# Attention and feed-forward emitted in the program's own order, one group of rows per step, instead of an order set by a scheduler

## The chip, the core and the metric

One core of a Trainium2 chip (four computing engines, here called PE for TensorE, DVE for VectorE, ACT for ScalarE and POOL for GpSimd, and SP, which only issues DMAs). The metric is device time in microseconds of one run of the whole program.

## What is computed

```python
# attention, B=4 batches, H=12 heads, S=448 rows, D=64
scores = q @ k.T / 8                       # per head
scores = einsum('bhij,hg->bgij', scores, w_pre)    # heads mixed before the softmax
attn   = softmax(scores)                           # exp(x - max) / (sum + 1e-9)
attn   = einsum('bhij,hg->bgij', attn, w_post)     # heads mixed after it
x      = (attn @ v)                        # to 1792 tokens x 768
# first feed-forward, d_ff 1536
x = (sigmoid(x @ w_gate) * (x @ w_val)) @ w_out
# second feed-forward, d_ff 2048
x = relu(x @ w_in) ** 2 @ w_out2
```

## The kernel before, in words

`attention` cuts each batch's 448 rows into four tiles (120, 120, 120 and 88 rows) and each tile into groups of ten rows: 12, 12, 12 and 9 groups, 45 a batch, 180 in all. Ten rows of twelve heads fill 120 partitions, so that one matmul mixes the heads of a whole group. Two tiles are a chunk. The work on TensorE is:

- `scores(n, p)`, 96 times: two heads of tile n against all keys, side by side in two halves of the array (64 rows of weights each); ACT copies the two results to `e`, and DMAs on SP's queue lay them out anew in `g`, rows by heads (two DMAs for a tile of 120 rows, four for one of 88).
- `premix(s)`, 180 times: one fp32 matmul of 448 columns, two passes in the trace; DVE takes the row maximum, `exponent(s)` on ACT makes exp and its sum, `normal(s)` takes two short steps on DVE and one on POOL (`wn`, the mixer scaled by 1/sum).
- `postmix(s)`, 180 times: four matmuls of 120 columns (eight passes); DVE copies the result into `ap` (`mixed`).
- `values(c, h)`, 48 times: two heads of a chunk, 240 or 208 columns, 16 passes in the other split of the array (64 columns each); ACT copies the result, and a DMA stores it to `xs`.

Premix uses two PSUM banks (`ps_m`), scores two (`ps_q`), postmix and values share four (`ps_b`). In the program a loop over `s` takes one group a step: premix of s, exponent of s-1, normal of s-2, postmix of s-3 or older, and scores of the next tile spread over the tile's steps. The work behind (postmix and values, the list `back`) is paced by a credit: `QUOTA` a step, `PW` or `VW` off it for each item.

That program order is only advice in the kernel before. Up to the end of attention the framework's scheduler puts each engine's instructions in an order of its own; `latest` and `issue_after` tie some instructions behind others. `mlp`, the feed-forward part, is a generator that attention feeds: for the last 40 groups (`EARLY`) it yields, and `whole` takes a step of `mlp` for each (weights loaded, split in parts that TensorE multiplies as fp32r: `w_bias`, `w_high`, `w_low`, `w_sum`, `w_round`, `w_rest`; then the activations `xh`, `xl`). What is left of `mlp` after attention is already emitted in the program's order (`manual_schedule`). It has 4896 matmuls of 448 columns (line 597), 36 for each block of weights.

Of the kernel before, what the change touches and what calls it, by code (L numbers as in the profile page):

```python
# [13 lines left out]
PSUM = bass.MemoryType.PSUM  # L14
DRAM = bass.MemoryType.DRAM

E = mybir.EngineType

P = 128
JP = 112  # L20
GI = 10
HV = 4
LAG = 3
LA = 3
NA = 8
PW, VW, QUOTA = 0.86, 1.6, 1.6
KB = 10
EARLY = 40
EM = 2
EACH = (1, 3, 2)  # L30
BEHIND = (E.Activation, E.DVE, E.Pool)


def row_tiles(S):
# [11 lines left out]
def attention(tc, q, k, v, w_pre, w_post, xs, B, H, S, D):  # L46
# [31 lines left out]
    with ExitStack() as ctx, ExitStack() as mid, ExitStack() as left:  # L78
# [15 lines left out]
        wp = one.tile([KM, GI, H], F32, name="wp")  # L94
        wq = one.tile([KM, H, GI], F32, name="wq")

        def mixers():
            wr = p0.tile([KM, 2, H], F32, name="wr")
            mask = p0.tile([KM, GI, H], F32, name="mask")
            for n, w in enumerate((w_pre, w_post)):  # L100
                nc.sync.dma_start(out=wr[:, n, :], in_=w.unsqueeze(0).to_broadcast([GI, H, H]))
            nc.gpsimd.memset(mask, 1.0)
            for base, mult in ((0, 1), (H - 1, -1)):
                nc.gpsimd.affine_select(
                    out=mask,
                    in_=mask,
                    compare_op=ALU.is_ge,
                    fill=0.0,
                    base=base,
                    pattern=[[-mult * H, GI], [0, H]],  # L110
                    channel_multiplier=mult,
                )
            nc.vector.tensor_tensor(
                out=wp, in0=mask, in1=wr[:, 0:1, :].to_broadcast([KM, GI, H]), op=ALU.mult
            )
            nc.vector.tensor_scalar(out=wp, in0=wp, scalar1=SCALE, scalar2=None, op0=ALU.mult)
            nc.vector.tensor_tensor(
                out=wq.rearrange("p g i -> p i g"),
                in0=mask,
                in1=wr[:, 1:2, :].to_broadcast([KM, GI, H]),  # L120
                op=ALU.mult,
            )
# [19 lines left out]
        def scores(n, p):  # L142

            b, i0, isz = tiles[n]
            if p == 0:
                g_t[n] = pg.tile([KM, GT, S], F32, tag="g", name="g")
            kt = k_t.pop((b, p)) if i0 + isz == S else k_t[b, p]
            ps = [
                ps_b.tile([P, S], F32, tag="b", name="ps_s")
                if n == 0 and p % 2  # L150
                else ps_q.tile([P, S], F32, tag="q", name="ps_s")
                for _ in range(2)
            ]
            for o in range(2):
                r = slice(o * D, (o + 1) * D)
                nc.tensor.matmul(  # L156
                    ps[o][:isz], lhsT=q_t[n][r, p, :isz], rhs=kt[r], start=True, stop=True
                )
            e = p4.tile([IM, 2, S], F32, tag="e", name="e")
            ng, rest = divmod(isz, GI)  # L160
            to = g_t[n].rearrange("(r h) g j -> h r g j", h=H)
            for o in range(2):
                if n == 0 and o:
                    nc.vector.tensor_copy(e[:isz, o], ps[o][:isz])
                else:
                    nc.scalar.copy(e[:isz, o], ps[o][:isz])  # L166
                for r0, r1, g in ((0, rest, ng + 1), (rest, GI, ng)):
                    if r0 < r1:
                        e0 = r0 * (ng + 1)
                        nc.sync.dma_start(  # L170
                            out=to[2 * p + o, r0:r1, :g], in_=e[e0 : e0 + (r1 - r0) * g, o]
                        )
# [4 lines left out]
        def premix(s):  # L177
            n, r0, rows = groups[s][:3]
            kk = rows * H
            ps = ps_m.tile([P, S], F32, tag="m", name="ps_m")  # L180
            w = wp.rearrange("p i g -> p (i g)")
            nc.tensor.matmul(  # L182
                ps[:kk], lhsT=w[:kk, :kk], rhs=g_t[n][:kk, r0 // GI], start=True, stop=True
            )
            nm = pa.tile([KM, 1], F32, tag="nm", name="nm")
            nc.vector.tensor_reduce(out=nm[:kk], in_=ps[:kk], op=ALU.max, axis=AX.X, negate=True)  # L186
            a_t[s] = [ps, nm]
# [86 lines left out]
        def load_next(load, order):  # L274
            x = next(order, None)
            if x is not None:
                load(*x)


        front = {s: [] for s in range(NG)}  # L280
        for n in range(1, NT):
            lo_, hi_ = starts[n - 1], starts[n] - LA
            for p in range(NP):
                front[lo_ + (hi_ - lo_) * p // NP].append((n, p))

        front_used = [s for s in front if front[s]]
        back = []
        for c, ch in enumerate(chunks):
            back += [(postmix, PW, s) for s in range(ch[3], ch[4])]
            back += [(values, VW, c, h) for h in range(0, H, 2)]  # L290
        bpos, credit = 0, 0.0

        def flush():
            now, pending[:] = list(pending), []
            for f, *x in now:
                f(*x)

        for p in range(0, NP, 2):
            q_load(0, p, p + 2)
            load_next(k_load, k_order)  # L300
            load_next(k_load, k_order)
        mixers()
        q_load(1)
        for p in range(NP):
            scores(0, p)
        with ExitStack() as behind:
            for ins in latest(tc, (mybir.EngineType.SP,)):
                behind.enter_context(tc.issue_after(ins))
            for _ in range(2):
                load_next(v_load, v_order)  # L310
            for _ in range(KB - NP):
                load_next(k_load, k_order)
        for s in range(NG + 30):
            if s < NG:
                premix(s)
            flush()
            if 1 <= s <= NG:
                exponent(s - 1)
            if 2 <= s < NG + 2:
                normal(s - 2)  # L320
            for n, h in front.get(s, ()):
                scores(n, h)
                if tiles[n][1] + tiles[n][2] == S:
                    load_next(k_load, k_order)
                if h == NP - 1 and n + 1 < NT:
                    q_load(n + 1)
            credit = min(credit, 0.0) + QUOTA
            fresh = None
            while bpos < len(back) and (credit > 0 or s >= NG):
                f, cost, *x = back[bpos]  # L330
                if f is postmix:
                    if x[0] > s - LAG:
                        break
                    fresh = groups[x[0]][3]
                elif x[0] == fresh:
                    if s < NG:
                        break
                    flush()
                if len(pending) > 3:
                    g, *y = pending.pop(0)  # L340
                    g(*y)
                f(*x)
                if f is values and (x[1] + 2) % HV == 0:
                    load_next(v_load, v_order)
                bpos += 1
                credit -= cost
                if f is postmix and x[0] == NG - 1:
                    flush()
                    mid.close()
                if s >= NG:  # L350
                    yield 3 if bpos == len(back) or back[bpos][0] is values else 2
            if s == max(front_used):
                left.close()
            if NG - EARLY <= s < NG:
                yield 1 if s < max(front_used) else 2
        flush()


# [337 lines left out]
@with_exitstack  # L696
def whole(ctx, tc, q, k, v, w_pre, w_post, wg, wv, wo, wi2, wo2, out):
    B, H, S, D = k.shape[0], 2 * k.shape[1], k.shape[3], k.shape[2] // 2
    DM = out.shape[0]
    dram = ctx.enter_context(tc.tile_pool(name="dram", bufs=1, space=DRAM))  # L700
    xs = [dram.tile([DM, S], F32, name=f"xs{b}") for b in range(B)]
    feed = mlp(tc, xs, wg, wv, wo, wi2, wo2, out, DM, wg.shape[0] * P, wi2.shape[0] * P)
    need = next(feed)
    for given in attention(tc, q, k, v, w_pre, w_post, xs, B, H, S, D):
        for _ in range(EACH[given - 1]):
            if need <= given:
                with ExitStack() as behind:
                    for ins in latest(tc, BEHIND):
                        behind.enter_context(tc.issue_after(ins))
                    need = next(feed)  # L710
    with tc.manual_schedule():
        for _ in feed:
            pass


def latest(tc, engines):

    found = {}
    for ins in reversed(tc.nc.cur_bb.bb.instructions):
        if ins.engine in engines and ins.engine not in found:  # L720
            found[ins.engine] = ins
            if len(found) == len(engines):
                break
    return list(found.values())


# [42 lines left out]
```

## Time and profile before

| what | us |
|---|---|
| median of 3 runs | 1574.31 (1571.27 to 1574.97) |
| the profiled execution | 1571.23 |
| its span in the profile | 1569.5 |
| from the start to the unbroken run of feed-forward matmuls | 604.74 |
| that run, 4714 of the 4896 | 961.25 |

A busy time of TensorE says little here: its matmuls are pipelined and the end of each is modelled, so two that follow with a small gap still look joined. What tells is the distance from the start of one piece to the start of the next.

### The profile page before, as it was taken

How to read it: one execution, taken by the hardware profiler on the slowest of the kernel's cores; microseconds unless marked ns; L12 is line 12 of the kernel's file. 1: busy time of each engine (PE TensorE's matmuls, PEld its weight loads, DVE VectorE, ACT ScalarE, POOL GpSimd, SP SyncE). 2: the span in 40 equal slices, each digit the busy share in tenths (PEclk: the TensorE clock that was granted, in tenths of full speed). 3: DMA queues.
4: the chain of work that ended last, by engine and by line, in shares of the span. 5: the costliest groups of instructions: out<-in, count | busy, mean ns of one | idle time of the engine just before them, and what ended most of it. 6: DMA issues, size and time to landing. Idle time of an engine off the chain costs nothing.

```text
span 1569.5 us, 21157 instructions
## 1 busy us (share of the span) xinstructions
PE 1510.5 (96%) x7848; PEld 1223.4 (78%) x7848; DVE 772.8 (49%) x1275; ACT 541.9 (35%) x1102; POOL 506.8 (32%) x403
## 2 busy tenths in 40 slices
PE   7889999899998899999999999999999999999999
PEld 3546555565554588999999999999999999999998
DVE  3535545473474648877888998961111100333000
ACT  3443444444453433333234443322222211333111
POOL 1211112121132335545455555542222222222221
PEclk8999999999999999999999999999999999999999
DMA  6334525244353334544444445641112121111221
GB/s 211 123 107 134 148 90 179 88 125 129 106 166 103 121 117 163 181 163 160 162 152 170 161 151 188 219 165 62 53 49 61 51 61 51 51 53 54 77 78 42
DMA packets 79530, 185.41 MB, mean 118 GB/s; under 512 B 11204, under 2 KB 48452, under 8 KB 79428
## 3 DMA queue, kind: packets, MB, share of 16 engines
q1 hardware_dynamic: 79428, 184.07, 36.4%
q8 instruction: 62, 1.02, 0.3%
q14 instruction: 40, 0.33, 0.1%
HBM read 107.75 MB, written 37.75 MB: 93 GB/s over the span
## 4 chain that ended last, share of the span: by engine, by line
PE 61%; DMA 0%; DVE 0%; POOL 0%; issue 0%; ACT 0%; ACTq 0%; DVEq 0%; SPq 0%; POOLq 0%
PE ps L597 61%; DMA w_raw<-in_wv 0%; POOL w L457 0%; POOL wl L470 0%; DVE w_t L439 0%; ACT w_f L417 0%; DVE w_f L446 0%; DVE w L426 0%; DVE w_t L423 0%; ACT o L629 0%; DVE ps L615 0%; DVEq L426 0%; ACTq L629 0%; SPq L407 0%; POOLq L457 0%
## 5 line engine op out<-in xcount | busy, mean ns | idle before, releaser
L470 POOL TENSOR_TENSOR wl<-w,wh 128x768 fp32r<-128x768 f32 (+1 forms) x140 | 259.3, 1854 | 543.8 <-ACT wh L464 537.8
L597 PE MATMUL ps<-xh,wl 128*128 128x448 f32 x960 | 350.9, 366 | 1.3 <-POOL wl L470 1.3
L597 PE MATMUL ps<-xh,wh 128*128 128x448 f32 x960 | 351.3, 366 | 0.1
L597 PE MATMUL ps<-xl,wh 128*128 128x448 f32 x960 | 350.9, 365 | 0.0
L597 PE MATMUL ps<-hh,wl 128*128 128x448 f32 x672 | 246.8, 367 | 0.0
L597 PE MATMUL ps<-hl,wh 128*128 128x448 f32 x672 | 246.8, 367 | 0.0
L597 PE MATMUL ps<-hh,wh 128*128 128x448 f32 x672 | 246.6, 367 | 0.0
L205 POOL TENSOR_SCALAR wn<-wq,sm 120x120 f32<-120x120 f32 x180 | 106.0, 589 | 427.3 <-DVE sm L203 256.4
L182 PE MATMUL ps_m<-g,wp 120*120 120x448 f32 x360 | 173.5, 580 | 29.3 <-ACT a L194 15.5
L220 PEld LDWEIGHTS ps_p<-wn,a 120*112 120x112 f32 (+1 forms) x1440 | 160.0, 177 | 49.0 <-issue 40.4
L597 PEld LDWEIGHTS ps<-xh,wl 128*128 128x128 f32 x960 | 180.3, 188 | 16.4 <-POOL wl L470 1.8
L597 PEld LDWEIGHTS ps<-xh,wh 128*128 128x128 f32 x960 | 180.3, 188 | 15.6 <-issue 0.6
L597 PEld LDWEIGHTS ps<-xl,wh 128*128 128x128 f32 x960 | 180.3, 188 | 14.8 <-issue 0.3
L186 DVE TENSOR_REDUCE nm<-ps_m 120x1 f32<-120x448 f32 x180 | 112.2, 623 | 145.4 <-PE ps_m L182 140.3
L194 ACT ACTIVATE a<-ps_m,nm 120x448 f32<-120x448 f32 x180 | 114.0, 633 | 197.0 <-DVE nm L186 126.4
L220 PE MATMUL ps_p<-wn,a 120*112 120x120 f32 (+1 forms) x1440 | 168.8, 269 | 3.1 <-POOL wn L205 2.8
L457 POOL TENSOR_TENSOR w<-w,w_f 128x768 f32<-128x768 f32 (+1 forms) x70 | 135.2, 1932 | 60.1 <-DVE w_f L446 60.1
L232 DVE COPY ap<-ps_p 112x480 f32<-112x480 f32 x180 | 117.1, 652 | 53.5 <-PE ps_p L220 47.8
L156 PE MATMUL ps_s<-k,q 64*120 64x448 f32 (+1 forms) x384 | 124.3, 614 | 15.1 <-ACT e L166 10.4
L597 PEld LDWEIGHTS ps<-hh,wh 128*128 128x128 f32 x672 | 126.1, 188 | 11.6
L597 PEld LDWEIGHTS ps<-hl,wh 128*128 128x128 f32 x672 | 126.1, 188 | 11.6
L597 PEld LDWEIGHTS ps<-hh,wl 128*128 128x128 f32 x672 | 126.1, 188 | 11.6
(39 smaller groups left out, 1291.8 us busy)
## 6 DMA issues: line engine op xcount, KB each, us to landing
g<-e SPq DMA_DIRECT2D x144, 210.0 KB
ws<-w SPq DMA_DIRECT2D x58, 384.0 KB
w<-ws SPq DMA_DIRECT2D x58, 384.0 KB
w_raw<-in_wo SPq DMA_DIRECT2D x18, 768.0 KB
w_raw<-in_wi SPq DMA_DIRECT2D x16, 768.0 KB
vraw<-in_v SPq DMA_DIRECT2D x24, 448.0 KB
w_raw<-in_wg SPq DMA_DIRECT2D x12, 768.0 KB
w_raw<-in_wv SPq DMA_DIRECT2D x12, 768.0 KB
```

The lines of the kernel that those rows point to most:

```text
L156: nc.tensor.matmul(ps[o][:isz], lhsT=q_t[n][r, p, :isz], rhs=kt[r], start=True, stop=True)
L182: nc.tensor.matmul(ps[:kk], lhsT=w[:kk, :kk], rhs=g_t[n][:kk, r0 // GI], start=True, stop=True)
L186: nc.vector.tensor_reduce(out=nm[:kk], in_=ps[:kk], op=ALU.max, axis=AX.X, negate=True)
L194: nc.scalar.activation(a[:kk], ps[:kk], AF.Exp, bias=nm[:kk], accum_out=sm[:kk])
L205: nc.gpsimd.tensor_scalar(out=wn[:kk], in0=wq[:kk], scalar1=sm[:kk], scalar2=None, op0=ALU.mult)
L220: nc.tensor.matmul(ps[:JP, jt], lhsT=a[:kk, jt * JP : (jt + 1) * JP], rhs=wn[:kk].rearrange("p g i -> p (g i)"), start=True, stop=True,)
L232: nc.vector.tensor_copy(ap[c][:, :, :, g0 - i0 : g0 - i0 + rows], ps[:JP, :, :, :rows])
L457: nc.gpsimd.tensor_tensor(out=x[:, s], in0=x[:, s], in1=fs.pop(n)[:, s], op=ALU.add)
L470: nc.gpsimd.tensor_tensor(out=lo[:, s], in0=w32.pop(n)[:, s], in1=h[:, s].bitcast(F32), op=ALU.subtract)
L597: nc.tensor.matmul(ps, lhsT=a, rhs=x, start=first and n == 0, stop=last and n == total - 1)
```

## The change

All of attention and the feed-forward part go under `manual_schedule`: each engine takes its instructions in the order in which the program emits them. The program's loop is laid out for that. The row maximum (`maximum`) is emitted after the copies of the step before. A step has a budget of `STEP` = 2.55, of which premix takes `MW`; scores of the next tile take `SW` where they are due, at most one a step, and one at the end of a step if there is room; the rest goes to postmix and values as long as over 0.5 is left. The load of `vraw` is held back to the next step's start. `mlp`'s early steps begin 64 groups before the end, one in every third step, until the scores are done. Nine buffers for the softmax's tiles instead of eight. `latest` and its ties are gone. The arithmetic is the same.

```diff
-NA = 8
-PW, VW, QUOTA = 0.86, 1.6, 1.6
+NA = 9
+MW, PW, VW, SW, STEP = 0.76, 0.82, 1.66, 1.04, 2.55
-EARLY = 40
+EARLY = 64
-EACH = (1, 3, 2)
-BEHIND = (E.Activation, E.DVE, E.Pool)
+EACH = (1, 2, 2)
...
+            a_t[s] = ps
+
+        def maximum(s):
+            kk, ps = groups[s][2] * H, a_t[s]
             nm = pa.tile([KM, 1], F32, tag="nm", name="nm")
             nc.vector.tensor_reduce(out=nm[:kk], in_=ps[:kk], op=ALU.max, axis=AX.X, negate=True)
...
             if s < NG:
                 premix(s)
             flush()
+            if s < NG:
+                maximum(s)
             if 1 <= s <= NG:
                 exponent(s - 1)
             if 2 <= s < NG + 2:
                 normal(s - 2)
-            for n, h in front.get(s, ()):
-                scores(n, h)
...
-            credit = min(credit, 0.0) + QUOTA
+            left_over = STEP - MW
+            ready = front and front[0][0] <= s
+            if ready and due(s):
+                next_scores()
+                ready, left_over = False, left_over - SW
             fresh = None
-            while bpos < len(back) and (credit > 0 or s >= NG):
+            while bpos < len(back) and (left_over > 0.5 or s >= NG):
...
                 if f is values and (x[1] + 2) % HV == 0:
-                    load_next(v_load, v_order)
+                    pending.append((load_next, v_load, v_order))
                 bpos += 1
-                credit -= cost
+                left_over -= cost
...
+            if ready and left_over > 0.4:
+                next_scores()
...
             if NG - EARLY <= s < NG:
-                yield 1 if s < max(front_used) else 2
+                if closed:
+                    yield 2
+                elif s % 3 == 0:
+                    yield 1
...
-    need = next(feed)
-    for given in attention(tc, q, k, v, w_pre, w_post, xs, B, H, S, D):
-        for _ in range(EACH[given - 1]):
-            if need <= given:
-                with ExitStack() as behind:
-                    for ins in latest(tc, BEHIND):
-                        behind.enter_context(tc.issue_after(ins))
+    with tc.manual_schedule():
+        need = next(feed)
+        for given in attention(tc, q, k, v, w_pre, w_post, xs, B, H, S, D):
+            for _ in range(EACH[given - 1]):
+                if need <= given:
                     need = next(feed)
-    with tc.manual_schedule():
         for _ in feed:
             pass
```

TensorE in the third batch, from the first values of its first chunk on. Before (ps_v is values, ps_s scores, ps_m premix, ps_p postmix; x8 of ps_v is one call of values, x4 of ps_p one of postmix, x2 of ps_s one of scores):

```order
L249 MATMUL ps_v<-ap,vraw 64x240 x32
L156 MATMUL ps_s<-k,q 88x448 x8
L182 MATMUL ps_m<-g,wp 120x448 x3
L156 MATMUL ps_s<-k,q 88x448
L182 MATMUL ps_m<-g,wp 120x448 x2
L156 MATMUL ps_s<-k,q 88x448
L182 MATMUL ps_m<-g,wp 120x448 x5
L156 MATMUL ps_s<-k,q 88x448 x2
L249 MATMUL ps_v<-ap,vraw 64x240 x16
L220 MATMUL ps_p<-wn,a 112x120 x8
```

The same place in the changed kernel:

```order
L253 MATMUL ps_v<-ap,vraw 64x240 x8
L182 MATMUL ps_m<-g,wp 120x448
L253 MATMUL ps_v<-ap,vraw 64x240 x8
L182 MATMUL ps_m<-g,wp 120x448
L253 MATMUL ps_v<-ap,vraw 64x240 x8
L182 MATMUL ps_m<-g,wp 120x448
L156 MATMUL ps_s<-k,q 88x448 x2
L253 MATMUL ps_v<-ap,vraw 64x240 x8
L182 MATMUL ps_m<-g,wp 120x448
L156 MATMUL ps_s<-k,q 88x448 x2
L253 MATMUL ps_v<-ap,vraw 64x240 x8
L182 MATMUL ps_m<-g,wp 120x448
```

Four values, four scores and runs of premixes in a row became single ones with a premix between each.

VectorE in the first tile, where a step has one premix and one postmix. Before:

```order
L232 COPY ap<-ps_p 112x48x10
L200 TENSOR_SCALAR sm<-sm 120x1
L186 TENSOR_REDUCE nm<-ps_m 120x1
L203 RECIPROCAL sm<-sm 120x1
L232 COPY ap<-ps_p 112x48x10
```

The same place in the changed kernel:

```order
L236 COPY ap<-ps_p 112x48x10
L190 TENSOR_REDUCE nm<-ps_m 120x1
L204 TENSOR_SCALAR sm<-sm 120x1
L207 RECIPROCAL sm<-sm 120x1
L236 COPY ap<-ps_p 112x48x10
```

The two short steps on `sm`, which belong to the group two before that of the maximum, moved behind that maximum.

## Rows read from the trace of the kernel before

**Rows 1.** The page: span, busy time of the engines, clock in 40 slices
```profile
span 1569.5 us, 21157 instructions
PE 1510.5 (96%) x7848; PEld 1223.4 (78%) x7848; DVE 772.8 (49%) x1275; ACT 541.9 (35%) x1102; POOL 506.8 (32%) x403
PEclk8999999999999999999999999999999999999999
```

**Rows 2.** The chain that ended last: start us, us, what
```profile
604.74 961.25 PE ps L597 x4714
...
1566.05 0.53 ACT o L629
```

**Rows 3.** Timeline of PE, values: start us, us, what, count [idle before <-releaser]
```profile
284.56 5.85 PE L249 MATMUL ps_v<-ap,vraw 112*64 112x208 f32 x64 [0.65 <-DVE ap L232]
...
353.10 6.70 PE L249 MATMUL ps_v<-ap,vraw 112*64 112x240 f32 x64 [0.75 <-DVE ap L232]
...
487.54 6.70 PE L249 MATMUL ps_v<-ap,vraw 112*64 112x240 f32 x64 [0.75 <-DVE ap L232]
```

**Rows 4.** Timeline of PE, premix and postmix in turn
```profile
276.01 0.98 PE L220 MATMUL ps_p<-wn,a 120*112 120x120 f32 x8
276.83 0.92 PE L182 MATMUL ps_m<-g,wp 120*120 120x448 f32 x2
277.59 0.98 PE L220 MATMUL ps_p<-wn,a 120*112 120x120 f32 x8
```

**Rows 5.** Timeline of PE, scores, postmix and premix in turn
```profile
331.29 1.02 PE L156 MATMUL ps_s<-k,q 64*120 64x448 f32 x4
332.23 1.07 PE L220 MATMUL ps_p<-wn,a 120*112 120x120 f32 x8
333.14 0.92 PE L182 MATMUL ps_m<-g,wp 120*120 120x448 f32 x2
333.99 1.02 PE L156 MATMUL ps_s<-k,q 64*120 64x448 f32 x4
```

**Rows 6.** Timeline of PE, values between two premixes
```profile
511.41 1.01 PE L182 MATMUL ps_m<-g,wp 120*120 120x448 f32 x2
512.35 1.84 PE L249 MATMUL ps_v<-ap,vraw 112*64 112x240 f32 x16
514.12 1.01 PE L182 MATMUL ps_m<-g,wp 120*120 120x448 f32 x2
```

**Rows 7.** Timeline of all engines, from a premix to a `wn`
```profile
299.14 1.01 PE L182 MATMUL ps_m<-g,wp 120*120 120x448 f32 x2 [0.78 <-ACT a L194]
...
300.19 0.62 DVE L186 TENSOR_REDUCE nm<-ps_m 120x1 f32<-120x448 f32 x1 [0.32 <-PE ps_m L182]
...
300.74 0.14 DVE L200 TENSOR_SCALAR sm<-sm 120x1 f32<-120x1 f32 x1
...
300.91 0.17 DVE L203 RECIPROCAL sm<-sm 120x1 f32<-120x1 f32 x1
...
301.27 0.58 POOL L205 TENSOR_SCALAR wn<-wq,sm 120x120 f32<-120x120 f32 x1 [0.62 <-PE ps_s L156]
```

**Rows 8.** Groups by line, `w_high`: what, count | busy us, mean ns | idle before
```profile
L426 DVE SCALAR_TENSOR_TENSOR w<-w_f,w_t 128x768 uint32<-128x768 uint32 (+1 forms) x70 | 109.1, 1559 | 6.1
L423 DVE TENSOR_SCALAR w_t<-w_f 128x768 uint32<-128x768 uint32 (+1 forms) x70 | 101.9, 1455 | 26.8 <-ACT w_f L417 24.9
```

**Rows 9.** Timeline of PE, scores of a tile and the first premix behind them
```profile
13.54 1.12 PE L156 MATMUL ps_s<-k,q 64*120 64x448 f32 x4 [1.66 <-ACT e L166]
...
24.15 4.86 PE L182 MATMUL ps_m<-g,wp 120*120 120x448 f32 x6
...
48.33 1.02 PE L156 MATMUL ps_s<-k,q 64*120 64x448 f32 x4
...
56.03 1.82 PE L182 MATMUL ps_m<-g,wp 120*120 120x448 f32 x2 [6.69 <-DMA q<-in_q]
...
534.16 3.24 PE L182 MATMUL ps_m<-g,wp 120*120 120x448 f32 x4 [3.47 <-DMA g<-e]
```

More of the change, by code (lines that the diff above doesn't have):

```diff
@@ L15 @@
 DRAM = bass.MemoryType.DRAM
-E = mybir.EngineType
 P = 128
@@ L95, in attention, with masks @@
         wq = one.tile([KM, H, GI], F32, name="wq")
-        def mixers():
-            wr = p0.tile([KM, 2, H], F32, name="wr")
-            mask = p0.tile([KM, GI, H], F32, name="mask")
+        wr = p0.tile([KM, 2, H], F32, name="wr")
+        mask = p0.tile([KM, GI, H], F32, name="mask")
+        def masks():
             for n, w in enumerate((w_pre, w_post)):
@@ L112, in mixers @@
                 )
+        def mixers():
             nc.vector.tensor_tensor(
@@ L277, in load_next, with due @@
                 load(*x)
-        front = {s: [] for s in range(NG)}
+        front = []
         for n in range(1, NT):
[L282 to L286, printed above, removed]
+            front += [(starts[n - 1], starts[n] - LA, n, p) for p in range(NP)]
+        def due(s):
+            return any(z - 1 - i <= s for i, (_, z, _, _) in enumerate(front[:NP]))
         back = []
@@ L290, in attention, with next_scores @@
             back += [(values, VW, c, h) for h in range(0, H, 2)]
-        bpos, credit = 0, 0.0
+        bpos, closed = 0, False
+        def next_scores():
+            _, _, n, h = front.pop(0)
+            scores(n, h)
+            if tiles[n][1] + tiles[n][2] == S:
+                load_next(k_load, k_order)
+            if h == NP - 1 and n + 1 < NT:
+                q_load(n + 1)
         def flush():
@@ L301, in attention @@
             load_next(k_load, k_order)
-        mixers()
+        masks()
         q_load(1)
@@ L305, in attention @@
             scores(0, p)
-        with ExitStack() as behind:
-            for ins in latest(tc, (mybir.EngineType.SP,)):
-                behind.enter_context(tc.issue_after(ins))
-            for _ in range(2):
-                load_next(v_load, v_order)
-            for _ in range(KB - NP):
-                load_next(k_load, k_order)
+        mixers()
+        for _ in range(2):
+            load_next(v_load, v_order)
+        for _ in range(KB - NP):
+            load_next(k_load, k_order)
         for s in range(NG + 30):
@@ L320, in attention @@
                 normal(s - 2)
-            for n, h in front.get(s, ()):
-                scores(n, h)
[L323 to L326, printed above, removed]
-            credit = min(credit, 0.0) + QUOTA
+            left_over = STEP - MW
[3 more added lines that the diff above has]
+                ready, left_over = False, left_over - SW
             fresh = None
-            while bpos < len(back) and (credit > 0 or s >= NG):
+            while bpos < len(back) and (left_over > 0.5 or s >= NG):
                 f, cost, *x = back[bpos]
@@ L339, in attention @@
                 if len(pending) > 3:
-                    g, *y = pending.pop(0)
-                    g(*y)
+                    flush()
                 f(*x)
                 if f is values and (x[1] + 2) % HV == 0:
-                    load_next(v_load, v_order)
+                    pending.append((load_next, v_load, v_order))
                 bpos += 1
-                credit -= cost
+                left_over -= cost
                 if f is postmix and x[0] == NG - 1:
@@ L351, in attention @@
                     yield 3 if bpos == len(back) or back[bpos][0] is values else 2
-            if s == max(front_used):
+            if ready and left_over > 0.4:
+                next_scores()
+            if not front and not closed:
                 left.close()
+                closed = True
             if NG - EARLY <= s < NG:
-                yield 1 if s < max(front_used) else 2
+                if closed:
+                    yield 2
+                elif s % 3 == 0:
+                    yield 1
         flush()
@@ L702, in whole @@
     feed = mlp(tc, xs, wg, wv, wo, wi2, wo2, out, DM, wg.shape[0] * P, wi2.shape[0] * P)
-    need = next(feed)
-    for given in attention(tc, q, k, v, w_pre, w_post, xs, B, H, S, D):
-        for _ in range(EACH[given - 1]):
-            if need <= given:
-                with ExitStack() as behind:
-                    for ins in latest(tc, BEHIND):
-                        behind.enter_context(tc.issue_after(ins))
+    with tc.manual_schedule():
[3 more added lines that the diff above has]
+                if need <= given:
                     need = next(feed)
-    with tc.manual_schedule():
         for _ in feed:
             pass
[L716 to L724, printed above, removed]
 def kernel(**inputs):
```

## The prediction
> **What bounds the kernel now.** I read the page first, then the chain that ended last, then TensorE's own timeline of attention. The page gives PE as busy for 1510.5 of 1569.5 us [rows 1], which sounds as if nothing could be gained, but those ends are modelled. The chain splits the run in two: from 604.74 us on TensorE runs 4714 feed-forward matmuls without a break for 961.25 us, 0.2039 us each, and only a copy and a store follow (3.5 us to the end of the span) [rows 2]. That part is already in program order and stays. Of the 4896 matmuls, 182 lie earlier, 182 x 0.2039 = 37.1 us, so attention and all its waits take 604.74 - 37.1 = 567.6 us. This is where the change acts.
>
> How long would attention be if TensorE never waited? Premix and postmix in turn take 0.76 and 0.82 us from start to start [rows 4], scores 0.94 [rows 5]; four values take 6.70 us with 240 columns and 5.85 with 208, so 1.66 and 1.44 each with the last one's tail taken off [rows 3]. A batch has 45 premixes, 45 postmixes, 24 scores, 6 wide and 6 narrow values: 45 x 1.58 + 24 x 0.94 + 6 x 1.66 + 6 x 1.44 = 112.3 us. Yet the same point of the third and the fourth batch lies 487.54 - 353.10 = 134.4 us apart [rows 3]. Some 22 us a batch are waits: values wait for DVE's last copy [rows 3], premixes in a row wait for the exp that frees one of their two banks, 0.78 us for each pair [rows 7], and a new tile's first premix waits for the scores' DMAs [rows 9].
>
> **The change, part by part.** The order shows that it does what it says: TensorE gets one premix a step and mixes the other kinds in between. From the changed order I counted 180 steps: 66 with premix, scores and postmix; 42 with premix and two postmixes; 26 with premix and one postmix; 21 with premix and values (12 wide, 9 narrow); 21 with premix, scores and values (12, 9); 3 with premix and scores at the start; and a last one with four postmixes and six values behind its premix.
>
> Their prices. Scores, postmix and premix in turn take 333.99 - 331.29 = 2.70 us, 0.18 more than 0.94 + 0.82 + 0.76: each change between scores and the rest costs about 0.1 [rows 5]. I use 2.71: 178.9 us. Premix and two postmixes are 0.76 + 2 x 0.82 = 2.40 [rows 4]: 100.8 us. Premix and wide values between premixes take 2.71 [rows 6], narrow 0.21 less [rows 3]: 32.5 + 22.5 us. With scores between, 0.85 + 0.95 + 1.77 = 3.57, narrow 3.36 [rows 5, 6]: 42.8 + 30.2 us. The three first steps 5.7, the last step 0.85 + 4 x 0.82 + 6 x 1.44 = 12.8.
>
> The 26 steps with one postmix would be 1.58, but there the new order bites. DVE now takes the short steps on `sm` only behind the maximum of the group two later. From that premix's start to the end of `wn` are 301.85 - 299.14 = 2.71 us [rows 7], 2.78 with the start of the postmix that needs it (my reading of the gap), and this postmix stands 0.76 behind the next premix. So such a step can't be shorter than 2.78 - 0.76 = 2.02: I take 2.03, 52.8 us in place of 41.1. The other kinds last longer than that and aren't held. Together the steps take 479.0 us.
>
> TensorE splits its array differently for scores and for values than for the mixers, and the new order has 246 changes of kind ahead of the feed-forward part where the old one had 169. The Trainium skill (TensorEngine Tiling (Array Packing), Key Properties) says that changing the tiling mode, not just the tile, drains the engine, which speaks against laying scores and values out singly. [Rows 5, 6] agree with about 0.1 us a change, and this is in the prices above; with free changes the steps would sum to 66 x 0.18 and about 0.25 for each of the 42 steps with values, some 22 us, less.
>
> Around the steps. The first premix needs the scores' DMAs: 48.33 + 1.02 to 56.03 is 6.7 us from the end of a tile's last scores to the next premix. The first tile's scores end at 14.66 [rows 9], so premix starts at about 21.3, and no longer behind four scores of the second tile as at 24.15. TensorE stands idle before it, and three premixes that tight take 2.4 took 4.86 there [rows 9], with the page's clock below full in that first slice [rows 1]: 2.5 us. The weights' preparation now falls into attention's DVE order: three `w_high` of 1.46 + 1.56 = 3.0 us [rows 8] and three smaller `w_low` are each queued ahead of a next step's copies and maximum, on which premix and postmix wait. All on the path that is about 15 us, none if the backlog of postmixes covers it (it does behind values): I take 8. The splitting of the activations (ACT and DVE in the last eleven steps), the last group's way through exp and `wn`, and the last `vraw` load, now issued a step later: between 0 and 15, I take 7.5. The hand-over to the feed-forward part: between 0 and a DMA's whole way of 6.7, I take 3.5.
>
> Edits at nothing: nine buffers instead of eight, and the ties taken away (a semaphore that is already up). The SP queue issues the same DMAs; those of scores now stand behind stores of values that wait for ACT. Their cover is the three steps or more between a tile's last scores and its first premix, 0.91 + 3 x 2.40 = 8.1 us against the 6.7 needed. If that is gone, see the second rival.
>
> Sum: 21.3 + 2.5 + 479.0 + 8 + 7.5 + 3.5 = 521.8 us, against 567.6: 45.8 us less. The profiled execution took 1571.23 us, so 1525.4; the median of the runs lies 3.1 above that execution, so 1528.5, say 1529.
>
> **Rivals.** *The small costs hide.* Weight loads overlap the changes of kind, the backlog covers the preparation and the ends: 22 + 8 + 7.5 us, and the 26 short steps run at 1.58 (12): 50 us more, 1479; half of it, 1504. For it: premix and postmix do run at 1.58 in the old order [rows 4]. Against it: rows 5 have the extra cost with no wait shown.
>
> *Slower: each tile waits for its scores.* In one SP queue the DMAs to `g` stand behind stores that wait for ACT, behind `vraw` and behind weight loads. If each of the 15 later tiles' first premixes waits the 3.47 us that one waited before [rows 9], that is 52 us: 1581. It decides from 45.8 / 15 = 3.1 us a tile. For it: 6.7 of 8.1 us are used already. Against it: the scores now come early, where before they came late in the tile.
>
> *ACT in program order.* In the 30 steps where scores come last, exp stands behind two copies that wait for those scores, and the next premix but one waits for that exp. If each costs the 0.78 us of rows 7, that is 23 us: 1552. Against it: premixes two steps apart, over 5 us, where in rows 7 they follow at once.
>
> **How the numbers follow.** The forecast 0.55 (1512 to 1545 by itself), small costs hidden 0.15, ACT 0.15, tiles waiting 0.10, and 0.05 that several of these eat just about all. The likeliest gives 1529. The range reaches halfway into the first rival and past ACT's: 1500 to 1563. About 0.3% (5 us) is what a measurement of this kernel tells from no change: faster by more 0.85, within 0.05, slower by more 0.10.
>
> **What would show it.** Right: the unbroken feed-forward run starts near 559 us in the new trace, wide values of the third and fourth batch lie about 120 us apart, steps with scores take 2.7, and the 26 short ones 2.0 with postmix waiting for `wn`. Wrong: premixes waiting for DMAs of `g` at tile starts, `exp` late behind copies, DVE busy with `w_high` while TensorE idles, or a feed-forward run that is no longer unbroken because its weights come too late.

## The result, and the profile after

The changed kernel takes 1529.41 us (median of four runs, 1528.61 to 1531.59) where the kernel before took 1572.95 beside it: a ratio of 0.9725, 95% interval 0.9707 to 0.9742, 2.7% faster. The prediction was 1529. The execution in the profile is the slowest of the four, 1531.59 us, against 1571.23 of before: 39.6 us less, where the sum had 45.8.

The page: the answer to [rows 1].

```profile
span 1529.9 us, 21163 instructions
PE 1491.3 (97%) x7848; PEld 1210.1 (79%) x7848; DVE 765.1 (50%) x1275; ACT 537.8 (35%) x1102; POOL 508.0 (33%) x403
PEclk8999999999999999999999999999999999999999
```

The chain that ended last (start us, us, what), the answer to [rows 2]. The unbroken feed-forward run begins 38.7 us sooner, and is 0.9 us shorter: all but that of the gain lies ahead of it, as forecast.

```profile
566.00 960.35 PE ps L612 x4714
```

TensorE's timeline where the second, third and fourth batch come to their first wide values, the answer to [rows 3] (the counts are cut by the window looked at):

```profile
206.96 0.83 PE L253 MATMUL ps_v<-ap,vraw 112*64 112x240 f32 x6
...
327.13 1.03 PE L253 MATMUL ps_v<-ap,vraw 112*64 112x240 f32 x8
...
459.24 1.02 PE L253 MATMUL ps_v<-ap,vraw 112*64 112x240 f32 x7
```

The same point of the second batch in the kernel before, to go with the third and the fourth in [rows 3]:

```profile
218.94 6.70 PE L249 MATMUL ps_v<-ap,vraw 112*64 112x240 f32 x64 [0.75 <-DVE ap L232]
```

From the second batch to the third are 120.2 us, where before they were 134.2 (and 134.4 from third to fourth). From the third to the fourth, for which the prediction had named 120, they are 132.1. So a batch is as fast as forecast, but not the one in which weights are loaded and prepared.

TensorE's timeline in undisturbed steps, the answer to [rows 4, 5, 6]: premix and two postmixes; premix, scores and postmix; premix and wide values.

```profile
284.46 0.92 PE L182 MATMUL ps_m<-g,wp 120*120 120x448 f32 x2
285.21 1.80 PE L224 MATMUL ps_p<-wn,a 120*112 120x120 f32 x16
286.85 0.92 PE L182 MATMUL ps_m<-g,wp 120*120 120x448 f32 x2
...
358.94 0.92 PE L182 MATMUL ps_m<-g,wp 120*120 120x448 f32 x2
359.78 1.02 PE L156 MATMUL ps_s<-k,q 64*120 64x448 f32 x4
360.73 1.07 PE L224 MATMUL ps_p<-wn,a 120*112 120x120 f32 x8
361.64 0.92 PE L182 MATMUL ps_m<-g,wp 120*120 120x448 f32 x2
...
331.62 1.01 PE L182 MATMUL ps_m<-g,wp 120*120 120x448 f32 x2
332.56 1.84 PE L253 MATMUL ps_v<-ap,vraw 112*64 112x240 f32 x16
334.33 1.01 PE L182 MATMUL ps_m<-g,wp 120*120 120x448 f32 x2
```

From premix to premix they take 2.39, 2.70 and 2.71 us; the sum used 2.40, 2.71 and 2.71. I took every step's length in this way, from the start of its premix to the start of the next, and put the 179 of them together by kind:

| kind of step | count | sum used, us | measured, us | undisturbed, each |
|---|---|---|---|---|
| premix, scores, postmix (either order) | 66 | 178.9 | 179.3 | 2.70 |
| premix, two postmixes | 42 | 100.8 | 110.8 | 2.39 |
| premix, postmix | 26 | 52.8 | 48.0 | 1.57 to 2.34 |
| premix, values | 21 | 55.0 | 55.1 | 2.71, 2.50 |
| premix, scores, values | 21 | 73.0 | 82.4 | 3.63, 3.45 |
| first three, at half speed in part | 3 | 8.2 | 8.3 | |

Two kinds are 10.0 and 9.4 us over. It isn't spread: steps 120, 123, 124, 141 and 142 are 12.0 us over their kind, 169 and 170 are 5.0 over. Steps 123 and 124 on TensorE and on ACT, and the windows' row (us, PE busy, PEld, DVE, ACT, POOL, granted clock, DMA share, GB/s) of two microseconds that begin 1.5 us behind the stall:

```profile
348.35 1.80 PE L224 MATMUL ps_p<-wn,a 120*112 120x120 f32 x16
352.51 1.85 PE L182 MATMUL ps_m<-g,wp 120*120 120x448 f32 x2 [2.35 <-ACT a L198]
354.15 2.56 PE L224 MATMUL ps_p<-wn,a 120*112 120x120 f32 x16
356.54 0.92 PE L182 MATMUL ps_m<-g,wp 120*120 120x448 f32 x2
...
351.47 0.36 ACT L268 COPY xo<-ps_v 128x240 f32<-128x240 f32 x1 [4.67 <-DMA xs<-xo]
351.72 0.64 ACT L198 ACTIVATE a<-ps_m,nm 120x448 f32<-120x448 f32 x1
...
354.00:356.00 2.00, 2.00 (x12) 1.85 (x11) 0.93 (x4) 0.73 (x2) 0.53 (x1) 0.58 0.68 152
```

ACT waits 4.67 us at a copy of values, since the buffer `xo` is still being stored; the exp stands behind that copy in ACT's order, and TensorE's premix needs the PSUM bank which that exp frees. TensorE idles 2.35 us. Then its granted clock is at the lower of its two levels for most of those two microseconds (0.58 on average), and premix and postmixes take 4.03 us in place of 2.39. So 2.35 us of idling cost 4.2.

The stalls of steps 120 and 141 begin in the same way, but what follows differs. TensorE's premix behind each, the windows' row behind the first, and the waits of premixes for exps in the whole run (in all, times, longest):

```profile
340.24 1.01 PE L182 MATMUL ps_m<-g,wp 120*120 120x448 f32 x2 [2.20 <-ACT a L198]
341.18 0.99 PE L156 MATMUL ps_s<-k,q 64*88 64x448 f32 x4
...
403.77 1.85 PE L182 MATMUL ps_m<-g,wp 120*120 120x448 f32 x2 [2.38 <-ACT a L198]
```

```profile
340.00:342.00 2.00, 1.76 (x6) 0.52 (x6) 0.69 (x2) 1.91 (x7) 0.00 (x0) 1.00 0.20 67
```

```profile
PE ps_m L182 <- ACT a L198: 10.1, 4, 3.1
```

Behind 2.20 us of idling the clock stayed at the higher level and the stall cost 2.3 us; behind 2.38 it fell, and steps 141 and 142 are 5.5 over.

The last stall, ACT and TensorE at steps 169 and 170:

```profile
484.27 0.56 ACT L546 CAST xh<-xr 128x448 fp32r<-128x448 f32 x1 [5.79 <-DMA xr<-xs]
...
485.51 1.85 PE L182 MATMUL ps_m<-g,wp 120*120 120x448 f32 x2 [3.13 <-ACT a L198]
```

Here it is an activation tile `xr` that comes late. The first premix of the fourth tile, step 36, and the scores behind it:

```profile
111.87 0.98 PE L182 MATMUL ps_m<-g,wp 120*120 120x448 f32 x2 [0.23 <-DMA q<-in_q]
113.36 1.02 PE L156 MATMUL ps_s<-k,q 64*120 64x448 f32 x4 [0.51 <-DMA q<-in_q]
```

The end of attention on TensorE, behind the last premix (506.67) and its postmixes:

```profile
513.91 5.85 PE L253 MATMUL ps_v<-ap,vraw 112*64 112x208 f32 x64 [0.65 <-DVE ap L236]
522.16 2.32 PE L253 MATMUL ps_v<-ap,vraw 112*64 112x208 f32 x16 [2.40 <-DMA vraw<-in_v]
```

From 506.67 to 566.00 are 59.3 us, of which 37.1 are the 182 feed-forward matmuls that come ahead of the unbroken run; 22.2 are the last step with its waits and the hand-over.

### The profile page after: what moved, and what is told of

It is laid out like the page before. It is cut to its first block, busy times and chain, and to the rows that moved or that the text cites. A ratio compares the mean times of both kernels' runs of the same rounds, so it can differ in the third digit from the quotient of the medians.

```text
span 1529.9 us, 21163 instructions
## 1 busy us (share of the span) xinstructions
PE 1491.3 (97%) x7848; PEld 1210.1 (79%) x7848; DVE 765.1 (50%) x1275; ACT 537.8 (35%) x1102; POOL 508.0 (33%) x403
## 4 chain that ended last, share of the span: by engine, by line
PE 63%; DMA 0%; DVE 0%; POOL 0%; issue 0%; ACT 0%; ACTq 0%; DVEq 0%; SPq 0%; POOLq 0%
PE ps L612 63%; DMA w_raw<-in_wv 0%; POOL w L472 0%; POOL wl L485 0%; DVE w_t L454 0%; ACT w_f L432 0%; DVE w_f L461 0%; DVE w L441 0%; DVE w_t L438 0%; ACT o L644 0%; DVE ps L630 0%; DVEq L441 0%; ACTq L644 0%; SPq L422 0%; POOLq L472 0%
## 5 line engine op out<-in xcount | busy, mean ns | idle before, releaser
L224 PEld LDWEIGHTS ps_p<-wn,a 120*112 120x112 f32 (+1 forms) x1440 | 164.6, 178 | 74.5 <-issue 46.4
L182 PE MATMUL ps_m<-g,wp 120*120 120x448 f32 x360 | 177.0, 574 | 22.4 <-DMA g<-e 11.9
L224 PE MATMUL ps_p<-wn,a 120*112 120x120 f32 (+1 forms) x1440 | 177.4, 271 | 3.5 <-POOL wn L209 3.2
L166 ACT COPY e<-ps_s 120x448 f32<-120x448 f32 (+1 forms) x186 | 90.0, 533 | 128.2 <-PE ps_s L156 107.9
```

The source lines that it names most:

```text
L182: nc.tensor.matmul(ps[:kk], lhsT=w[:kk, :kk], rhs=g_t[n][:kk, r0 // GI], start=True, stop=True)
L224: nc.tensor.matmul(ps[:JP, jt], lhsT=a[:kk, jt * JP : (jt + 1) * JP], rhs=wn[:kk].rearrange("p g i -> p (g i)"), start=True, stop=True,)
```

## Experiments

Ratios are against the kernel before on the same chip; 1% is 15.7 us.

**Which half of the change gains?** The order without the new layout: the program text of before, all of it under `manual_schedule`, with the ties gone.

```diff
...
-                with ExitStack() as behind:
-                    for ins in latest(tc, BEHIND):
-                        behind.enter_context(tc.issue_after(ins))
+    with tc.manual_schedule():
+        need = next(feed)
+        for given in attention(tc, q, k, v, w_pre, w_post, xs, B, H, S, D):
...
```

> The program text of the kernel before, with its own step layout and pacing, but every engine takes its instructions in program order, and the ties are gone. Theory (the scheduler's bunching of values, scores and premixes was the loss; any order with a premix between the others removes it): most of the gain, 1530 to 1545 us; its TensorE order has 47 steps of premix and one postmix instead of 26, some 6 us more than the changed kernel. Rival (the layout in steps with a budget is what gains, and program order alone stalls on engines that are queued badly): within 10 us of before, 1562 to 1582.

Measured: 1543.53 us (1542.11 to 1544.98), ratio 0.9808 (0.9793 to 0.9824). And the layout without the order: the changed program's text, with the scheduler and the ties of before (the same lines with + and - exchanged).

> The changed kernel's step layout, constants and emission order, with the scheduler left to order the engines up to the end of attention, and the ties of the kernel before. Theory: the scheduler bunches again (four values, eight scores passes in a row stand in its order), so 1562 to 1580 us, no gain. Rival (the layout gains by itself): 1530 to 1545.

Measured: 1588.76 us (1586.29 to 1591.9), ratio 1.0098 (1.0075 to 1.0121), slower than before, and slower than I had allowed. TensorE's timeline in this kernel shows the scheduler putting pieces of a kind together again:

```profile
373.53 0.99 PE L159 MATMUL ps_s<-k,q 64*88 64x448 f32 x4
375.13 1.42 PE L159 MATMUL ps_s<-k,q 64*88 64x448 f32 x4 [0.61 <-ACT e L169]
...
389.23 1.76 PE L185 MATMUL ps_m<-g,wp 120*120 120x448 f32 x4 [0.78 <-ACT a L201]
```

Scores behind scores wait for ACT's copies, and premixes come in pairs that wait 0.78 for the exp, as in [rows 7]. So the order alone gives 1.92% of the 2.75%, and the layout gives its 0.83% only on top of it; by itself it costs 1%. Premixes waited 21.9 us for exps here, against 15.5 in the kernel before. Why the scheduler does worse with this text than with the old one, I did not take further apart. Nor did I run the ties apart from the order, or the parts of the layout (budget, nine buffers, earlier start of `mlp`) apart from each other.

**What stalls steps 120 to 142?** Four buffers for the values on their way out, in a pool of their own, in place of two.

```diff
+        po = ctx.enter_context(tc.tile_pool(name="a_o", bufs=4, **kw))
...
-            xo = pv.tile([P, CM], F32, tag="xo", name="xo")
+            xo = po.tile([P, CM], F32, tag="xo", name="xo")
```

> The changed kernel with four buffers instead of two for xo, the copy of the values that a DMA stores. In the changed kernel's trace five steps right behind the three weight loads that lie in attention (steps 120, 123, 124, 141, 142 of 180) are 11.9 us too long in sum; ACT's xo copy waits there for the store of two values earlier to land, and exp and the next premix queue behind it. Theory (the store lands late behind 768 KB of weights, and ACT waits in order): those waits go, 8 to 12 us less than the changed kernel, 1517 to 1522. Rival (DVE's w_high, as the prediction had it): no change, 1527 to 1531.

Measured: 1521.22 us (1518.94 to 1524.32), ratio 0.9668 (0.9648 to 0.9687). Steps 123 and 124 take 2.49 and 2.39, the 21 steps of scores and values 74.8 us in place of 82.4. DVE still prepares the weights there, and none of the steps 115 to 152 is more than 0.22 over its kind, so this isn't what held them: the store is. Why is it late? The stalled steps follow the issue of weight loads of 768 KB. To tell, no weight tile is loaded or prepared in those steps:

```diff
         for n, k in enumerate(early):
-            advance(k)
             yield 1 if n + 1 < len(early) else 2
```

> The changed kernel, but no weight tile is loaded or prepared during the steps of attention until the activations are; their slots stay empty, and the work is done at the end. Theory (values' stores land late behind the three 768 KB weight loads, and ScalarE's next copy of values waits for its buffer): steps 120, 123, 124, 141 and 142 take what their kind takes (3.63, 2.39, 2.39, 3.45, 3.45 us; in the changed kernel they take 11.9 us more together), and no wait of that copy for its store is left. Rival (the values' own stores and loads do it, without the weights): the same steps stay late by 8 us or more. The end pays for it in either case: the feed-forward part waits for the first weights, some 10 to 15 us, so the time is near the changed kernel's 1529, between 1524 and 1538.

Measured: 1533.70 us beside 1574.07 of before, one run of each, so without an interval. Steps 120, 123, 124, 141 and 142 took 3.63, 2.49, 2.39, 3.45 and 3.45. ACT's waits from 40 to 500 us (in all, times, longest), of the changed kernel and of this one:

```profile
ACT xo L268 <- DMA xs<-xo: 19.8, 4, 6.5
```

```profile
ACT xo L268 <- DMA xs<-xo: 5.1, 2, 2.8
```

The 5.1 us that are left, against what I expected, are two waits of 2.2 and 2.8 us far ahead of the weights, and no step of values is longer for them. So without the weights the stores are not late. This run takes the loads and their preparation away together; that it is the loads is argued from the wait, which is for a store in the same queue. What I had priced as DVE's work shows no cost: in the changed kernel's DVE timeline `w_high` lies between two steps' copies, beside the undisturbed scores step shown above, and the step behind it takes 2.70 too.

```profile
360.69 0.54 DVE L438 TENSOR_SCALAR w_t<-w_f 128x768 uint32<-128x768 uint32 x1
361.27 1.00 DVE L441 SCALAR_TENSOR_TENSOR w<-w_f,w_t 128x768 uint32<-128x768 uint32 x1
```

The last premix starts at 497.51 in this kernel, 9.2 us sooner than in the changed one, and the end takes more than that back, waiting for the weights.

**Why are the short steps 1.85 and not 2.03?** `normal` of the group two back is put ahead of the maximum on DVE.

```diff
+            if 2 <= s < NG + 2:
+                normal(s - 2)
             if s < NG:
                 maximum(s)
...
-            if 2 <= s < NG + 2:
-                normal(s - 2)
```

> The changed kernel with normal(s-2) emitted ahead of maximum(s) in each step, so that DVE takes the two short steps on sm before the row maximum. Theory (the 26 steps with one postmix last 1.85 us in place of 1.58 because wn comes behind the maximum): these steps fall to 1.58 to 1.65, 5 to 7 us less, 1522 to 1525. Rival (they are bound by DVE's sum of copy, maximum and short steps, or by ACT): no change, 1528 to 1531.

Measured: 1523.38 us (1518.51 to 1524.36), ratio 0.9674 (0.9654 to 0.9694). TensorE's timeline in short steps of this kernel:

```profile
70.08 0.92 PE L182 MATMUL ps_m<-g,wp 120*120 120x448 f32 x2
70.83 0.98 PE L224 MATMUL ps_p<-wn,a 120*112 120x120 f32 x8
71.65 0.92 PE L182 MATMUL ps_m<-g,wp 120*120 120x448 f32 x2
```

From premix to premix 1.57, the price without waits. So the maximum ahead of `normal` did hold such steps, as the prediction said: 16 of the 26 now take 1.57 or 1.58. But steps 68 and 113 went from 1.81 and 1.86 to 2.27 and 2.33 and step 175 from 2.34 to 3.12, for which I have no cause, so all 26 gain 2.2 us and not the 5 to 7 expected. The same stretch of the changed kernel, all engines:

```profile
69.88 0.92 PE L182 MATMUL ps_m<-g,wp 120*120 120x448 f32 x2
...
70.83 0.62 DVE L190 TENSOR_REDUCE nm<-ps_m 120x1 f32<-120x448 f32 x1
71.38 0.14 DVE L204 TENSOR_SCALAR sm<-sm 120x1 f32<-120x1 f32 x1
...
71.62 0.92 PE L182 MATMUL ps_m<-g,wp 120*120 120x448 f32 x2
...
71.91 0.58 POOL L209 TENSOR_SCALAR wn<-wq,sm 120x120 f32<-120x120 f32 x1 [1.25 <-PE ps_p L224]
```

`wn` ends 72.49 - 69.88 = 2.61 us behind the premix's start (the prediction read 2.71 from [rows 7]), and the postmix that needs it starts at 72.55, 0.93 behind the next premix and not 0.76: that premix didn't wait with it. The loop closes over two steps: 2.67 from premix to postmix and some 0.9 from there to the next premix but one, 3.6 for two steps, 1.8 each. The two runs of six such steps measured 1.76 and 1.81 on average.

The kernel gains 8.0 us by ratio; the 26 steps explain 2.2 (45.8 in place of 48.0), and the steps of scores and values 3.8 (78.6 in place of 82.4), whose stalls came out shorter. The rest is about the width of the interval. So the total fell where expected partly by luck.

**What holds steps 169 and 170?** The activation tiles are loaded four slots ahead of their split, not two, in four buffers of their own.

```diff
+        pxr = pool("m_xr", 4, side="left")
...
-            xr[c, i] = pf.tile([P, N], F32, tag="xr", name="xr")
+            xr[c, i] = pxr.tile([P, N], F32, tag="xr", name="xr")
...
-                for n in range(len(todo) + 2):
-                    if n >= 2:
-                        x_split(hf, *todo[n - 2])
+                for n in range(len(todo) + 4):
+                    if n >= 4:
+                        x_split(hf, *todo[n - 4])
```

> The changed kernel, with each activation tile loaded four slots ahead of its split in place of two, in four buffers of their own. In the changed kernel ScalarE waited 5.79 us for such a load in the steps around 484 us, and two steps took 4.9 us more than their kind. Theory (ScalarE takes the cast in its place and everything behind it is late): this wait goes, the steps from 165 on take what their kind takes, and the unbroken feed-forward run starts 4 to 8 us sooner, near 560; the time is near 1524 us, 0.969 of the kernel before. Rival (the load itself is slow there because the queue is full, and the wait moves to the next reader): no gain, 1529 us.

Measured: 1524.14 us (1521.90 to 1528.16), ratio 0.9686 (0.9667 to 0.9704), 6 us less than the changed kernel by the ratios, whose intervals lie just apart. The theory is half right: step 169 is undisturbed, but the first cast still waits 4.00 us for its tile, step 170 is 1.3 over its kind, and 173 to 176, where the casts now fall, are 3.8 longer in sum than in the changed kernel. In the profile the unbroken run starts at 562.52, 3.5 us sooner, a little less than the 4 to 8 expected.

**All three edits together.**

> The changed kernel with three edits together: four buffers for the values on their way out, normal of two groups back ahead of the maximum, and the activation tiles loaded four slots ahead. If the three costs are separate, the gains add: 8.2 us by the first alone, 6.0 by the second, some 5 by the third, so near 1510 us, 0.960 of the kernel before, with a feed-forward run from about 546 us. If they cover each other (a postmix that comes earlier only waits elsewhere), the best of them is all that is left: 1520 us. By the first rival of the prediction, which would have 1504 with half of the small costs hidden, this is about where it ends.

Measured: 1514.18 us (1511.09 to 1518.66), ratio 0.9622 (0.9601 to 0.9643): faster than both kernels, 1.0% below the changed one. The single gains by ratio are 9.0, 8.0 and 6.1 us, 23 together; 16 come out, between the two cases expected (1510 and 1520 us), so they cover each other in part. The chain that ended last in this kernel:

```profile
549.33 960.36 PE ps L614 x4714
```

**What does a change between ways of splitting the array cost?** One matmul over all 128 rows for a scores unit, where the kernel has two on 64 rows each, both copies reading its bank. The scores of two heads are summed by it, so this kernel computes something else.

```diff
-                for _ in range(2)
-            ]
-            for o in range(2):
-                r = slice(o * D, (o + 1) * D)
-                nc.tensor.matmul(
-                    ps[o][:isz], lhsT=q_t[n][r, p, :isz], rhs=kt[r], start=True, stop=True
-                )
+                for _ in range(1)
+            ] * 2
+            nc.tensor.matmul(
+                ps[0][:isz], lhsT=q_t[n][:, p, :isz], rhs=kt, start=True, stop=True
+            )
```

> The changed kernel with one matmul over all 128 rows for a scores unit in place of two on 64 rows each; both copies read its bank, so the scores of two heads are summed and this part of the computation is changed. Everything else stays. The step of premix, scores and postmix takes 2.70 us in the changed kernel, 0.18 more than 0.76 + 0.94 + 0.82. Theory (changing how the array is split costs 0.1 us each way): a scores unit takes 0.76 like a premix and the step 2.34, some 0.36 less in each of 87 steps, 31 us in all if no other engine becomes the bound: between 1498 and 1510 us. Rival (the 0.18 comes from the order, whatever the shape): the step stays at 2.52 or more, at most 16 us less, 1513 us or more.

Measured: 1507.67 us (1502.39 to 1509.79), ratio 0.9573 (0.9552 to 0.9594). TensorE's timeline of premix, scores and postmix:

```profile
233.92 0.92 PE L180 MATMUL ps_m<-g,wp 120*120 120x448 f32 x2
234.67 0.92 PE L154 MATMUL ps_s<-k,q 128*120 128x448 f32 x2
235.43 0.98 PE L222 MATMUL ps_p<-wn,a 120*112 120x120 f32 x8
236.25 0.92 PE L180 MATMUL ps_m<-g,wp 120*120 120x448 f32 x2
```

A step takes 2.33 us, 0.75 + 0.76 + 0.82, nothing on top. So the 0.18 us that scores have over their own 0.94 goes with the split, and so does the 0.18 between 0.94 and 0.76; the run takes the split and the second matmul away together, and does not tell which of them makes the latter. 55 of the 66 steps take 2.33; steps 36 and 81 take 4.76 and 4.31, with waits for DMAs and matmuls at half speed. The 66 steps lose 19.2 us, the steps with values 6.2, the run as a whole 24 by the ratios; I had expected up to 31, with 0.36 in every step, but next to values only 0.16 goes (3.63 to 3.47), presumably as a change into the values' split stays. The two changes around a scores unit come to 0.09 us each. The Trainium skill (TensorEngine Tiling (Array Packing), Key Properties) says that a change of the tiling mode drains the engine. The runs agree as far as each change costs time.

**When does the slower rival come true?** The last scores of a tile two steps later.

```diff
-LA = 3
+LA = 1
```

> The changed kernel with the last scores of a tile two steps later: one step of 3.2 us (three times 2.4) lies between the end of a tile's last scores and the tile's first premix, in place of 5.6 to 8.9, for 13 of the 15 later tiles. By the slower rival of the prediction (a tile's first premix waits for its scores to come back through memory, 6.7 us), each waits 3.5 to 4.3 us: 10 x 3.5 + 3 x 4.3 = 48 us, 1577 us, slower than the kernel before. If the way is shorter than 6.7, as the tiles with 5.6 us of cover seem to say, 35 to 45 us: 1564 to 1574. If postmixes make up for it (no wait on the path): 1529.

Measured: 1599.98 us (1596.79 to 1601.53), ratio 1.0168 (1.0151 to 1.0185): slower than before, by more than any theory had. TensorE at step 36, and SP's own queue ahead of it:

```profile
116.45 1.82 PE L182 MATMUL ps_m<-g,wp 120*120 120x448 f32 x2 [6.12 <-DMA q<-in_q]
118.07 2.66 PE L224 MATMUL ps_p<-wn,a 120*112 120x120 f32 x16
```

```profile
105.60 2.89 SPq L170 DMA_DIRECT2D g<-e  x4
...
109.04 3.48 SPq L170 DMA_DIRECT2D g<-e  x4
```

The premix reads `g` and not `q`; I take the wait, which the profile puts down to the DMA issued last, for one on `g`. Two prices were missing. First, the way from a tile's last scores to its first premix is 6.1 to 7.4 us for nine of the 13 tiles, as assumed, but 8.2 to 10.2 for the four whose scores have 88 rows: those take four DMAs a unit, which keep SP's queue for 2.9 to 3.5 us, longer than the step of 2.7 in which the next unit comes. Second, each wait is followed by matmuls at half speed, as 1.82 and 2.66 in place of 0.92 and 1.80 show. In the profile the unbroken run starts 65.2 us later than in the changed kernel, 5.0 for each of the 13 tiles; by the waits of premixes some 4.1 of that are idle time (65.6 us less 12.6 for the very first premix, in 13 parts); that the rest follows the clock is argued.

## Why the prediction came out, and where its steps did not

The number is right within 0.4 us, and part of that is luck. The sum gave 1525.4 for the profiled execution, which took 1531.6, 6.2 more; I had added 3.1 to come to the median, but this time the profiled execution lies 2.2 above its median. In the trace, attention without the 182 matmuls takes 566.0 - 37.1 = 528.9 us where the sum had 521.8, 7.1 more, and the unbroken run gives 0.9 of it back.

| term | sum, us | measured, us |
|---|---|---|
| first premix | 21.3 | 22.8 |
| steps, undisturbed, with the first ones at half speed | 468.7 | 466.9 |
| weights' preparation | 8 | 12.0 |
| activations, last step and group, `vraw`, hand-over (7.5 + 12.8 + 3.5) | 23.8 | 27.2 |
| sum | 521.8 | 528.9 |

- **Where the time goes.** Right: the run of 961 us stays, the gain lies ahead of it, and a batch without weights takes 120 us. The two signs that the prediction named for this did not come so: the run begins at 566.0 and not near 559, and the third and fourth batch lie 132.1 and not 120 apart, since the stalls of 12.0 us lie between them. Reading the prices of pieces from start to start in the old trace, and counting the kinds of steps in the new order, gave 138 of the 150 steps of the other four kinds (without the short ones and the first three) within 0.1 us; seven of the other twelve are the stalls.
- **Half speed at the start.** Right: 8.3 for the first three steps, 8.2 expected. That the same can come back behind a stall in the middle I had not said: it did behind three of the four waits of premixes for exps, which make 10.1 of the 17.0 us that the stalls cost, and not behind the one of 2.20 us.
- **The 26 short steps.** Right that the maximum ahead of `normal` holds them, as moving it showed; wrong in size. I let the waiting postmix stand 0.76 behind the premix of its step, as an unhindered one does. It stands 0.93 behind it, since the premix is not held by the wait. Closing the loop over two steps, 2.78 + 0.82 = 3.60 by the prediction's own rows, gives 1.80 a step, near the 1.76 and 1.81 of the runs of six. 4.8 us too much.
- **Steps of scores and values.** 3.57 and 3.36 used, 3.63 and 3.45 measured. The term that was too small is the premix: I took 0.85 to the scores from [rows 5], where it stands behind a postmix, but here it stands behind values, and takes 0.94 (340.24 to 341.18 in step 120), the length that [rows 6] have.
- **Weights' preparation.** Nearly the size, and the wrong mechanism. I had priced DVE, and put the queue of stores under "edits at nothing", with only the scores' DMAs in mind. The price was wrong too: the two instructions of a `w_high` take 0.54 and 1.00 us here, where I had taken 3.0 from the mean of the whole run. What cost 12.0 us is, three times, a store of values that lands late while weights of 768 KB are on their way: it keeps a buffer, the buffer holds ACT's copy, the copy holds the exp behind it. In program order nothing may pass it. Giving the values more buffers or taking the weights away ends it.
- **Activations and hand-over.** A wait of the same kind, on a load (5.0 us), which the price had not named; the last `vraw` load did cost 2.4, as named.
- **Rivals.** "Small costs hide" came in one part: DVE's preparation of the weights shows no cost. The changes of split are paid for, since a step of scores without them is the plain sum of its pieces. "Each tile waits for its scores" came once, and small: the premix of step 36 is 0.4 late. Steps 36 and 81 themselves are 0.65 and 0.37 too long because scores wait there for `q`, 0.51 in step 36. (The profile puts that premix's own wait down to `q` too, though it reads `g`.) But with two steps less of cover the kernel is slower than before: the price of 3.47 a tile was too low there, 5.0 was paid. "ACT in program order" came in another shape than the one priced: not the copies of scores, but the copies of values that wait for a store.

## What to carry to other kernels

An engine in program order makes each wait of one instruction a wait of all behind it, so look not only at what an engine does in a step but at what its slowest buffer waits for, and at what else is in that DMA queue. If a loop of waits goes through two steps, close it over two steps before dividing. And fixing the order and laying out the program for it are one edit: apart, one gave 70% of the gain here and the other lost 1%.

## What the runs showed of the hardware

- An idle gap of 2.35 us on TensorE cost 4.2 in all, since the granted clock averaged 0.58 in two microseconds that followed, near the lower of its two levels (1.2 of 2.4 GHz), and a premix took 1.85 in place of 0.92. Behind a gap of 6.12 us a premix took 1.82. Behind one of 2.20 us the clock stayed at 1.00 and a premix took 1.01, as it does behind values.
- A scores unit of two matmuls on two halves of the array takes 0.94 us and 0.18 in changes, where one matmul on the whole array with the same columns takes 0.76 and none.
- Four DMAs of a scores unit of 88 rows keep SP's queue busy for 2.9 to 3.5 us, longer than the step of 2.7 us that issues them: a limit that no busy row of the page shows.
